# The first search of a routed expert layer in a written order, later routing steps, and weights requested in parts

## The chip, the cores and the metric

The kernel runs on one core of a Trainium2 chip. The metric is the device time of one execution in microseconds. Five engines work side by side, each through its own list of instructions in order: TensorE (PE; its weight loads are drawn apart as PEld), VectorE (DVE), ScalarE (ACT), GpSimd (POOL) and SyncE (SP), which issues most of the DMA transfers. They meet at semaphores.

## The reference

First a gated linear attention over q, k, v, alpha of 4 batches, 8 heads, 768 steps, head size 48:

```
state = alpha_t[:, None] * state + outer(k_t, v_t)      # 48 x 48 for each batch and head
y_t   = q_t @ state
```

Its output, laid out as x of 3072 tokens by 384, goes to a layer of 8 experts, each of which takes 384 tokens:

```
logits = x @ w_gate                                  # 3072 x 8
for idx in argsort(-logits.flatten()):               # best pair first
    tok, e = divmod(idx, 8)
    if assigned[tok] < 0 and counts[e] < 384: assigned[tok] = e; counts[e] += 1
out[mask_e] = relu(x[mask_e] @ w1[e]) @ w2[e]        # w1: 384 x 1024, w2: 1024 x 384
```

The assignment is greedy over 24,576 pairs. Which expert fills up first, and so which pairs are struck out, depends on the data.

## The kernel before

**Attention.** 24 steps (6 groups of 512 tokens by 4 pairs of heads) build the output channel by channel. Each result must be turned by four 128x128 transposes on TensorE (`y_trans`, L340), copied from PSUM by ScalarE into a tile `xg`, and stored to `x_dram` once a group of four steps is whole (L350). Eight of these 24 turnings are done by `fill` inside the attention part; sixteen are left.

**Routing.** In place of a sort the kernel finds, eight times, the expert that fills up next. `search` looks for the threshold key in five digits of 7, 7, 6, 6, 6 bits. A level compares all keys with all digit values (`compare`, the tables `cmp`, on VectorE), counts by expert with 24 small matmuls (`counts`), marks which digits reach the remaining capacity (`reached`), and sums the marks into the next digit (`flags`, whose result is `k`; then `next_digit`). `find` names the expert, and requests its weights on SyncE's queue with an address read from a register; `offsets` and `places` number its tokens; `one_hot` and `index` turn the numbers into a list of rows; `gather` brings the rows from `x_dram` by three indirect DMAs on GpSimd. `take_places`, `best_left`, `left` and `new_choice` strike the full expert out and choose anew. Level 0 of the first search is worked out during attention (`g0`).

**Order of the first search.** Attention is written under an order set by hand. The first `search(0)` is not: the planner orders it, with constraints that hold each level's counts behind the flag before and behind a given number of turnings (`Y_IN_SEARCH = (3, 4, 4, 3)`: 3, 4, 4 and 3 turnings, of four transposes each). All sixteen turnings come ahead of it in the program.

**Products.** Each expert makes 8 units `ffn1(i, q)` (9 matmuls of 384 columns, hidden block q) and 8 units `ffn2(i, [q])` (9 matmuls into three output banks): 144 products. Both operands are split into a high part on ScalarE (`split_hi`, `XH` in `rows`) and the rest on GpSimd (`split_lo`) or VectorE (`rows_lo`, `hl`), so each block takes three products. `rows(i, b)` turns the gathered block b of 128 tokens.

**The plan.** TensorE, VectorE, ScalarE and GpSimd run an order written out by hand. `products` gives the 1152 products one by one; a list `plan` says ahead of which product number each routing step of the next expert is written. Expert i's group of steps starts at `base`: 76 for i = 1, then 209, 342, 486, 630, 774 and 814, with 133, 133, 144, 144, 144 and 40 products between. From expert 2 on, the first unit of the expert is placed ahead of the last unit of the one before (L894). `spin_more` writes matmuls without a use, whose number is in `SPIN`.

**Weights.** `weights` requests the first half of an expert's w1 and w2 (four of eight hidden blocks) and, for all experts but the first, the other half at once. The first expert's other half is requested when its rows have landed (`second_half`).

Of the kernel before, what the change touches and what calls it, by code (L numbers as in the profile page):

```python
# [17 lines left out]
Y_IN_SEARCH = (3, 4, 4, 3)  # L18
SPIN = (16, 0, 4, 3, 3)
TRI = 11  # L20
HOT = 24
# [10 lines left out]
def gla_moe_kernel(ctx, tc, q, k, v, alpha, w_gate, w1, w2, out):  # L32
# [112 lines left out]
    NS = NG * HP  # L145
    psx = ctx.enter_context(tc.tile_pool(name="psx", bufs=1, space=bass.MemoryType.PSUM))
# [4 lines left out]
    pst = att.enter_context(tc.tile_pool(name="pst", bufs=1, space=bass.MemoryType.PSUM))  # L151
    ps = att.enter_context(tc.tile_pool(name="ps", bufs=1, space=bass.MemoryType.PSUM))
# [86 lines left out]
    def turned():  # L239
        turn[0] = not turn[0]  # L240
        return (psx if turn[0] else pst).tile([128, 4, C], F32, name="xt")

    turn = [False]
# [94 lines left out]
    YM = {}  # L338

    def y_trans(s):  # L340
        g, p = divmod(s, HP)
        o = turned()
        for u in range(4):
            YM[s] = nc.tensor.transpose(o[:, u], YT[s][:, u], ident)  # L344
        if p == 0:
            XG[g] = ytp.tile([128, 4, Dm], F32, name="xg", bufs=2)
        nc.scalar.activation(XG[g][:, :, 2 * D * p:2 * D * p + 2 * D].rearrange("p u (h d) -> p u h d", h=2),
                             o.rearrange("p u (h d) -> p u h d", h=2)[:, :, :, :D], AF.Copy)
        if p == HP - 1:
            nc.scalar.dma_start(x_dram[4 * g * C:4 * (g + 1) * C].rearrange("(u p) d -> p u d", p=C), XG[g])  # L350
# [68 lines left out]
    late = list(range(NS))  # L419

    def fill(n):
        for _ in range(min(n, len(late))):
            y_trans(late.pop(0))
# [62 lines left out]
    head = [NS - len(late)]  # L486
    fill(NS)
    att.close()

    rw = ctx.enter_context(tc.tile_pool(name="route_work", bufs=2))  # L490
    wp = ctx.enter_context(tc.tile_pool(name="weights", bufs=2))
    fp = ctx.enter_context(tc.tile_pool(name="ffn", bufs=2))
    fpt = ctx.enter_context(tc.tile_pool(name="ffn_pst", bufs=1, space=bass.MemoryType.PSUM))
    fps = ctx.enter_context(tc.tile_pool(name="ffn_ps", bufs=1, space=bass.MemoryType.PSUM))

# [14 lines left out]
    ab_c, q0_c, bi_c = slot(NU), slot(NU), slot(NU, I32)  # L510
    un_c, key_c, wi_c = ab_c, q0_c.bitcast(I32), v1_c.bitcast(I32)
    nc.vector.tensor_copy(ramp_c, ramp)
    nc.vector.tensor_copy(cst_c, cst)
# [12 lines left out]
    second_half = []  # L526

    def weights(i, ei):
# [4 lines left out]
        def half(hf):  # L533
            fs = slice(hf * F // 2, (hf + 1) * F // 2)
            a = nc.sync.dma_start(W1R[i][:, :, fs], w1v[bass.ds(ev, 1), :, :, fs].rearrange("e p c f -> p (e c) f"))
            qs = slice(hf * FB // 2, (hf + 1) * FB // 2)
            b = nc.sync.dma_start(W2R[i][:, qs], w2v[bass.ds(ev, 1), :, qs].rearrange("e p c d -> p (e c) d"))
# [18 lines left out]
    def halves(i):  # L556
        return [slice(0, NU // 2), slice(NU // 2, NU)] if i == 0 else [slice(0, NU)]
# [3 lines left out]
    last_k = [None]  # L561

    def search(i):
        chu, o, dig = st["chu"], st["o"], st["dig"]
        st["d"] = dig[0]
        for t, bits in enumerate(BITS):
            if t == 0:
                g = g0
            else:
                g = rw.tile([128, E], BF, name="g")  # L570
                final = t == nb - 1
                rt = st["rt"] = fps.tile([128, 64], F32, name="rt")
                cnt = rt[:, 32:40]
                head[0] += Y_IN_SEARCH[t - 1]
                order = [last_k[0], YM[head[0] - 1]]
                for cmp, js in compare(i, st["d"], t, final):
                    with ExitStack() as es_:
                        for x in order:
                            es_.enter_context(tc.issue_after(x.ins))
                        for j in range(js.start, js.stop):  # L580
                            nc.tensor.matmul(cnt, cmp[:, j // U, :, j % U], o[:, j], start=(j == 0), stop=(j == NU - 1))
                nc.vector.tensor_tensor(g, cnt, rem, op=OP.is_ge)
                if final:
                    keep_counts()
            if t == 0:
                st["rt"] = fps.tile([128, 64], F32, name="rt")
            st["g"] = g
            flags(t)
            if t < nb - 1:
                next_digit(t)  # L590

    def keep_counts():
        st["nt"] = nt = 2 ** BITS[-1]
        st["cs"] = rw.tile([128, E], F32, name="cs")
        nc.vector.tensor_copy(st["cs"][:nt + 1], st["rt"][:nt + 1, 32:40])

    def flags(t):
        rt = st["rt"]
        last_k[0] = nc.tensor.matmul(rt[:, :8], onet[t], st["g"], start=True, stop=True)
        st["k"] = rw.tile([128, 1], F32, name="k")  # L600
# [335 lines left out]
    with tc.manual_schedule(engines={E_.DVE, E_.PE, E_.Activation, E_.Pool}):  # L936
# [27 lines left out]
        for n in (3, 4):  # L964
            split_lo(0, n)
# [118 lines left out]
```

## Time and profile before

| | |
|---|---|
| median of 3 runs | 433.83 us (433.4 to 434.31) |
| profiled execution | 433.69 us, its span 431.8 us |
| TensorE busy | 396.6 us, 92% of the span |
| VectorE busy | 284.2 us, 66% |
| GpSimd busy | 279.9 us, 65% |
| ScalarE busy | 195.7 us, 45% |
| mean granted TensorE clock | 0.969 |
| last flag of the first search | 149.29 us |
| first product | 165.65 us |

Times in a profile row are the start from the span's beginning and the duration, in us. In a timeline row stand the start, the duration, the engine, the line of the kernel, the operation, the tiles (out<-in), shapes and a count; in brackets the idle time of the engine ahead of it and what ended it. A row with a count above one has several instructions merged. In a waits row stand who waited, for whom, the total in us, the times and the longest.

### The profile page before, as it was taken

How to read it: one execution, taken by the hardware profiler on the slowest of the kernel's cores; microseconds unless marked ns; L12 is line 12 of the kernel's file. 1: busy time of each engine (PE TensorE's matmuls, PEld its weight loads, DVE VectorE, ACT ScalarE, POOL GpSimd, SP SyncE). 2: the span in 40 equal slices, each digit the busy share in tenths (PEclk: the TensorE clock that was granted, in tenths of full speed). 3: DMA queues.
4: the chain of work that ended last, by engine and by line, in shares of the span. 5: the costliest groups of instructions: out<-in, count | busy, mean ns of one | idle time of the engine just before them, and what ended most of it. 6: DMA issues, size and time to landing. Idle time of an engine off the chain costs nothing.

```text
span 431.8 us, 10887 instructions
## 1 busy us (share of the span) xinstructions
PE 396.6 (92%) x4154; PEld 347.8 (81%) x4154; DVE 284.2 (66%) x838; ACT 195.7 (45%) x447; POOL 279.9 (65%) x327
## 2 busy tenths in 40 slices
PE   7999999989898858989999999999999997999993
PEld 3787777768676737989898899999999887999993
DVE  7888888878736497686697597687587576221210
ACT  1476666556565422424423534434434433644411
POOL 4668988677620026854687786776866865997802
PEclk9699999999999769999999999999999999999998
DMA  8999966660004584180180190191191198310101
GB/s 284 331 270 263 255 193 206 179 188 18 2 3 169 197 264 160 54 295 2 31 317 20 47 330 28 44 329 35 40 326 38 39 325 304 106 71 2 55 2 55
DMA packets 34467, 63.39 MB, mean 147 GB/s; under 512 B 3328, under 2 KB 14592, under 8 KB 34416
## 3 DMA queue, kind: packets, MB, share of 16 engines
q1 hardware_dynamic: 28176, 48.54, 36.0%
q0 software_dynamic: 3072, 9.44, 6.3%
q10 hardware_dynamic: 3168, 4.72, 3.1%
q8 instruction: 33, 0.54, 0.5%
q14 instruction: 18, 0.15, 0.1%
HBM read 53.25 MB, written 9.44 MB: 145 GB/s over the span
## 4 chain that ended last, share of the span: by engine, by line
PE 62%; DVE 21%; issue 6%; DMA 4%; POOL 3%; ACT 2%; SPq 0%; DVEq 0%; POOLq 0%; ACTq 0%
PE h L835 17%; PE y L855 16%; PE rt L614 6%; PE y L312 4%; PE y L306 4%; PE s L257 4%; DVE ga L226 3%; DVE sc L221 2%; DVE cmp L552 2%; PE xt L344 2%; DVE hot L699 2%; PE xt L249 2%; DMA raw_a<-in_alpha_dram 2%; PE xt L818 2%; PE xt L708 2%
## 5 line engine op out<-in xcount | busy, mean ns | idle before, releaser
L799 POOL TENSOR_TENSOR wlo<-w1r,whi 128x384 fp32r<-128x384 f32 x64 | 69.2, 1082 | 24.1 <-ACT whi L790 22.4
L799 POOL TENSOR_TENSOR wlo<-w2r,whi 128x384 fp32r<-128x384 f32 x64 | 68.0, 1063 | 25.6 <-PE xt L818 9.5
L840 ACT ACTIVATE hh<-h 128x384 fp32r<-128x384 f32 x64 | 31.5, 492 | 110.7 <-PE h L835 105.0
L841 DVE SCALAR_TENSOR_TENSOR hl<-h,hh 128x384 fp32r<-128x384 f32 x64 | 35.4, 553 | 51.8 <-ACT hh L840 50.6
L855 PE MATMUL y<-whi,hl 128*128 128x384 f32 x192 | 65.8, 343 | 0.0
L855 PE MATMUL y<-wlo,hh 128*128 128x384 f32 x192 | 65.8, 343 | 0.0
L855 PE MATMUL y<-whi,hh 128*128 128x384 f32 x192 | 64.9, 338 | 0.0
L716 POOL DMA_INDIRECT xr<-x_dram,idx x24 | 29.5, 1229 | 44.2 <-DVE asg L746 32.2
L269 POOL TENSOR_SCALAR_AFFINE_SELECT sm<-sm 128x512 f32<-128x512 f32 x48 | 29.4, 639 | 31.8 <-ACT sm L265 31.8
L835 PE MATMUL h<-xh,whi 128*128 128x384 f32 x192 | 47.5, 346 | 0.1
L835 PE MATMUL h<-xh,wlo 128*128 128x384 f32 x192 | 46.0, 344 | 0.0
L835 PE MATMUL h<-xl,whi 128*128 128x384 f32 x192 | 46.0, 344 | 0.0
L790 ACT ACTIVATE whi<-w1r 128x384 fp32r<-128x384 f32 x64 | 33.3, 520 | 25.0 <-PE y L855 10.8
L290 ACT ACTIVATE sb<-st,sc 128x48 f32<-128x48 f32 x80 | 24.6, 331 | 35.6 <-DVE st L297 21.2
L872 POOL DMA_INDIRECT out_dram<-yt,idx x24 | 25.0, 1043 | 18.4 <-ACT yt L859 14.6
L855 PEld LDWEIGHTS y<-whi,hl 128*128 128x128 f32 x192 | 36.2, 188 | 0.1
L855 PEld LDWEIGHTS y<-wlo,hh 128*128 128x128 f32 x192 | 36.2, 188 | 0.0
L855 PEld LDWEIGHTS y<-whi,hh 128*128 128x128 f32 x192 | 36.1, 188 | 0.0
L835 PEld LDWEIGHTS h<-xh,whi 128*128 128x128 f32 x192 | 33.6, 189 | 0.5 <-ACT xh L819 0.5
L835 PEld LDWEIGHTS h<-xh,wlo 128*128 128x128 f32 x192 | 33.8, 189 | 0.0
L552 DVE TENSOR_TENSOR cmp<-nd,iota 128x1536 bf16<-128x1536 bf16 (+4 forms) x32 | 33.1, 1044 | 1.0
L835 PEld LDWEIGHTS h<-xl,whi 128*128 128x128 f32 x192 | 33.6, 189 | 0.0
(177 smaller groups left out, 808.8 us busy)
## 6 DMA issues: line engine op xcount, KB each, us to landing
w1r<-in_moe_w_dram SPq DMA_DIRECT2D x16, 768.0 KB, 4.8
w2r<-in_moe_w_dram SPq DMA_DIRECT2D x16, 768.0 KB, 6.2
vt<-in_v_dram SPq DMA_DIRECT2D x24, 256.0 KB, 4.8
x_dram<-xg ACTq DMA_DIRECT2D x6, 768.0 KB, 3.7
raw_a<-in_alpha_dram SPq DMA_DIRECT2D x19, 226.2 KB
raw_k<-in_k_dram SPq DMA_DIRECT2D x19, 224.0 KB
raw_q<-in_q_dram SPq DMA_DIRECT2D x19, 224.0 KB, 5.2
raw_a<-in_alpha_dram SPq DMA_DIRECT2D x5, 258.5 KB, 5.0
```

Of the source, the lines that this page charges most:

```text
L269: nc.gpsimd.affine_select(SM[s][:, h], SM[s][:, h], pattern=[[0, 4], [1, C]], compare_op=OP.is_ge, fill=0.0, base=0, channel_multiplier=-1)
L290: nc.scalar.activation(SB[s, u][:, :D], St[p], AF.Copy, scale=ac)
L552: x = nc.vector.tensor_tensor(words(dst, nt, js), keyed(d, nt, js), each(iotas[t], nt, js), op=OP.is_ge)
L614: nc.tensor.matmul(rt[:, 32:40], st["cmp"][:, j // U, :, j % U], st["o"][:, j], start=(j == 0), stop=(j == NU - 1))
L716: g = nc.gpsimd.indirect_dma_start(out=XR[i][:, b], out_offset=None, in_=x_dram, in_offset=bass.IndirectOffsetOnAxis(ap=IDX[i][:, b:b + 1] ...
L790: nc.scalar.activation(hi[:, 0], a, AF.Copy)
L799: y = nc.gpsimd.tensor_sub(lo[:, h], x[h], hi[:, h])
L835: nc.tensor.matmul(o, a[:, 0, d], x[:, d], start=(n == 0), stop=(n == 3 * DB - 1))
L840: nc.scalar.activation(hh, o, AF.Relu)
L841: nc.vector.scalar_tensor_tensor(hl, o, 0.0, hh, op0=OP.max, op1=OP.subtract)
L855: nc.tensor.matmul(Y[b], a[:, bs], w[:, 1].rearrange("p a b -> p (a b)"), start=(q == 0 and n == 0), stop=(q == FB - 1 and n == 2))
L872: st_ = nc.gpsimd.indirect_dma_start(out=out, out_offset=bass.IndirectOffsetOnAxis(ap=IDX[i][:, b:b + 1], axis=0), in_=yts.pop((i, b)), in ...
```

## The change

It has five parts.

1. The first search is written into the hand-made order (`search_first`). A turning is now four steps of one transpose each (`y_steps`; the fourth brings the copy and, at the end of a group, the store). Three steps come ahead of each flag, 11, 8, 8 and 8 behind the flag and ahead of the counts of levels 1 to 4; the rest comes behind the last flag. The table is made in parts of 16 and 8 columns in place of 12 and 12. The tiles of the search lie in a pool of their own (`levels`), attention's tiles are let go only behind it, and `xg` has three buffers. The transposes alternate between `psx` and the bank of `y1`.
2. The bank `rt` of counts and flags is one tile throughout.
3. The first expert: two of eight blocks are split early in place of four, `spin_more` gives 16, 1, 1, 2 matmuls in place of 16, 4, 3, 3 (one more place had none), and level 0's flag and the steps behind it come after the third block of rows. The masking of `L` moves from `take_places`, ahead of the indices on VectorE, to `best_left`, behind them.
4. New positions: bases 98, 238, 382, 526, 670, 814, 872; other offsets for levels, places, one-hot, rows and splits. The table of level 0 comes behind `new_choice`. The first unit of an expert is no longer moved ahead of the last unit of the one before.
5. Weights: the first expert's come in parts of 2, 2 and 4 blocks, the others' in 4 and 4; all but the first part are requested when the expert's gathered rows have landed (`later`).

```
-Y_IN_SEARCH = (3, 4, 4, 3)
-SPIN = (16, 0, 4, 3, 3)
-TRI = 11
-HOT = 24
+Y_IN_LEVEL = (None, 11, 8, 8, 8)
+Y_BEFORE_FLAGS = 3
+SPIN = (16, 0, 1, 1, 2)
...
-        half(0)
-        if i:
-            half(1)
-        else:
-            second_half.append(half)
+        cuts = (0, 2, 4, FB) if i == 0 else (0, 4, FB)
+        part(*cuts[:2])
+        for lo, hi in zip(cuts[1:], cuts[2:]):
+            later.append((part, lo, hi))
...
+    def search_first():
+        st["d"] = st["dig"][0]
+        st["g"] = g0
+        steps(Y_BEFORE_FLAGS)
+        nc.vector.tensor_copy(ramp_c, ramp)
+        nc.vector.tensor_copy(cst_c, cst)
+        flags(0)
+        for t in range(1, nb):
+            next_digit(t - 1)
+            parts = list(compare(0, st["d"], t, t == nb - 1))
+            steps(Y_IN_LEVEL[t])
+            for cmp, js in parts:
+                for j in range(js.start, js.stop):
+                    nc.tensor.matmul(rt[:, 32:40], cmp[:, j // U, :, j % U], st["o"][:, j],
+                                     start=(j == 0), stop=(j == NU - 1))
+            reached(t)
+            steps(Y_BEFORE_FLAGS)
+            flags(t)
+        steps(4 * NS)
...
-            if i > 1:
-                units.insert(len(units) - 1, mine.pop(0))
...
+        if t == 0:
+            at(base + 11, rows_lo, i - 1, 1)
         if t < nb - 1:
-            at(base + 2, next_digit, t)
-            at(base + 2, table, i, t + 1)
+            at(base + (2 if t else 11), next_digit, t)
+            at(base + (2 if t else 11), table, i, t + 1)
...
-        levels(0, 1, {1: 1, 2: 9, 3: 21, 4: 36}, {})
-        found(39, 1, 37)
+    levels(0, 1, {1: 15, 2: 28, 3: 41, 4: 55}, {})
+    found(57, 1, 41)
...
-            loose = i > 2
-            offs = {0: 35, 1: 52, 2: 68, 3: 84, 4: 100} if loose else {0: 33, 1: 49, 2: 64, 3: 79, 4: 94}
-            end = 144 if loose else 133
+        offs = dict(enumerate((33, 56, 69, 83, 97) if i == 1 else (33, 57, 71, 85, 99)))
+        end = 140 if i == 1 else 144
...
-            at(base + 31, rows, i, 0)
-            at(base + (48 if loose else 45), rows, i, 1)
-            at(base + (60 if loose else 57), rows, i, 2)
+        for b, p in enumerate((31, 40, 46) if i == 1 else (31, 41, 50)):
+            at(base + p, rows, i, b)
...
-                at(base + 20, offsets, i + 1)
+            at(base + 34, offsets, i + 1)
```

More of the change, by code (lines that the diff above doesn't have):

```diff
@@ L417, in first @@
                                  ga[:, 129 * u:129 * u + 258].rearrange("p (g x) -> p g x", x=129)[:, :, 1:])
-    late = list(range(NS))
+    late = (x for s in range(NS) for x in y_steps(s))
     def fill(n):
-        for _ in range(min(n, len(late))):
-            y_trans(late.pop(0))
+        for _ in range(4 * n):
+            next(late, None)
     def run(seq):
@@ L485, in gla_moe_kernel @@
         first_counts(NG - 1)
[L486 to L493, printed above, removed]
+    first_psum.close()
     fps = ctx.enter_context(tc.tile_pool(name="ffn_ps", bufs=1, space=bass.MemoryType.PSUM))
+    spare_bank[0] = fps
     scr = fps.tile([128, 512], F32, name="scr")
@@ L556, in halves @@
     def halves(i):
-        return [slice(0, NU // 2), slice(NU // 2, NU)] if i == 0 else [slice(0, NU)]
+        return [slice(0, 2 * NU // 3), slice(2 * NU // 3, NU)] if i == 0 else [slice(0, NU)]
     st = dict(chu=chu0, o=o0, dig=[dig0[:, t] for t in range(nb)])
[L561 to L587, printed above, removed]
@@ L588, in search, with steps @@
             flags(t)
-            if t < nb - 1:
-                next_digit(t)
+        steps(4 * NS)
+    def steps(n):
+        for _ in range(n):
+            next(late, None)
     def keep_counts():
         st["nt"] = nt = 2 ** BITS[-1]
-        st["cs"] = rw.tile([128, E], F32, name="cs")
-        nc.vector.tensor_copy(st["cs"][:nt + 1], st["rt"][:nt + 1, 32:40])
+        st["cs"] = sm.tile([128, E], F32, name="cs")
+        nc.vector.tensor_copy(st["cs"][:nt + 1], rt[:nt + 1, 32:40])
     def flags(t):
-        rt = st["rt"]
@@ L718, in gather @@
                 in_offset=bass.IndirectOffsetOnAxis(ap=IDX[i][:, b:b + 1], axis=0))
-        for half in second_half:
-            for d_ in half(1):
+        for part, lo, hi in later:
+            for d_ in part(lo, hi):
                 tc.add_manual_dep(d_.ins, g.ins.name,
                                   mybir.DependencyInfo(mybir.DependencyClass.Sync, mybir.DependencyReason.DATA),
-                                  reason="rows of the first expert before its later weights")
-        second_half.clear()
+                                  reason="an expert's rows before its later weights")
+        later.clear()
     def take_places(i):
@@ new lines, in gla_moe_kernel @@
+    written = tc.manual_schedule(engines={E_.DVE, E_.PE, E_.Activation, E_.Pool})
+    written.__enter__()
+    search_first()
+    att.close()
+    rw = ctx.enter_context(tc.tile_pool(name="route_work", bufs=2))
+    wp = ctx.enter_context(tc.tile_pool(name="weights", bufs=2))
+    fp = ctx.enter_context(tc.tile_pool(name="ffn", bufs=2))
+    find(0)
+    offsets(0)
+    places(0)
+    one_hot(0)
+    index(0)
+    take_places(0)
+    gone()
+    spin_more(SPIN[0])
+    gather(0)
+    best_left(0)
@@ new lines, in gla_moe_kernel @@
+    left(0)
+    new_choice(0)
+    table(1, 0)
+    for q in range(2):
+        split_hi(0, q)
+    for n in range(3):
+        split_lo(0, n)
+    rows(0, 0)
+    counts(0)
+    rows_lo(0, 0)
+    reached(0)
+    spin_more(SPIN[2])
+    rows(0, 1)
+    rows_lo(0, 1)
+    spin_more(SPIN[3])
+    rows(0, 2)
+    flags(0)
+    rows_lo(0, 2)
+    next_digit(0)
+    table(1, 1)
+    split_hi(0, 2)
+    for n in (3, 4):
+        split_lo(0, n)
+    split_hi(0, 3)
+    spin_more(SPIN[4])
+    levels(0, 1, {1: 15, 2: 28, 3: 41, 4: 55}, {})
@@ L1044, with catch_up @@
+    plan.sort()
+    waiting, made = [], products()
+    def catch_up():
+        waiting[:] = [(fn, args) for fn, args in waiting if fn(*args) is False]
+    for n in range(2 * E * FB * NB * DB):
+        while plan and plan[0][0] <= n:
+            waiting.append(plan.pop(0)[2:])
+        catch_up()
+        next(made)
+    for _ in made:
+        pass
+    catch_up()
+    assert not waiting and not plan
+    written.__exit__(None, None, None)
 _INS = ["q", "k", "v", "alpha", "moe_w_gate", "moe_w1", "moe_w2"]
```

232 lines of the change are left out of this document (91 added, 141 removed).

## The prediction

> **What bounds the kernel now.** I read the page first, then the busy time by stage, then TensorE's waits in the expert stage, then the timeline of the stretch between attention and the first product.
>
> ```profile
> span 431.8 us, 10887 instructions
> ...
> L841 DVE SCALAR_TENSOR_TENSOR hl<-h,hh 128x384 fp32r<-128x384 f32 x64 | 35.4, 553 | 51.8 <-ACT hh L840 50.6
> ...
> x_dram<-xg ACTq DMA_DIRECT2D x6, 768.0 KB, 3.7
> ```
>
> The profiled execution took 433.69 us, 0.14 under the median of the three runs; its span is 431.8, so 1.9 us lie around it. Sums below are made against 433.69.
>
> Busy time by stretch (PE, PEld, DVE, ACT, POOL, then the granted clock, DMA share, GB/s):
>
> ```profile
> 140.00:142.00 2.00, 2.00 (x31) 1.94 (x31) 0.17 (x1) 0.91 (x2) 0.00 (x0) 0.50 0.93 332
> ...
> 152.00:154.00 2.00, 0.00 (x0) 0.00 (x0) 1.83 (x8) 0.00 (x0) 0.00 (x0) 0.60 1.03 319
> ...
> 134.05:149.29 15.24, 13.63 (x157) 11.58 (x156) 7.66 (x24) 6.66 (x14) 0.00 (x0) 0.78 0.51 182
> 149.29:165.65 16.36, 10.30 (x97) 6.90 (x95) 13.53 (x51) 5.82 (x13) 5.99 (x6) 0.79 0.71 219
> ...
> 285.00:318.00 33.00, 32.82 (x307) 30.49 (x305) 24.16 (x74) 13.61 (x30) 24.38 (x26) 1.00 0.38 129
> ```
>
> Three stages matter. The first search (134 to 149) runs partly at half clock, TensorE busy with transposes. From 149 to 166 VectorE sets the pace (13.5 of 16.4 us busy). After that TensorE does: one expert's 33 us hold 32.8 of it. So whatever moves there counts only through TensorE's waits, and these are few:
>
> ```profile
> PE rt L663 <- DVE rts L653: 2.7, 1, 2.7
> PE rt L659 <- DVE rts L640: 2.1, 3, 1.1
> PE xt L708 <- DVE rhs L701: 1.5, 3, 0.7
> PE rt L614 <- DVE cmp L552: 1.3, 3, 0.7
> PE xt L818 <- DVE rem L775: 0.6, 1, 0.6
> PE xt L708 <- DVE xl L824: 0.3, 1, 0.3
> PE xt L818 <- DVE xl L824: 0.2, 1, 0.2
> PE xt L818 <- DVE chu L769: 0.2, 1, 0.2
> ```
>
> That is 14 waits, 8.9 us idle. A product is drawn as some 0.34 us but they start 0.173 apart, so each wait hides another 0.17: 8.9 + 14 x 0.17 = 11.3 us in all. This is the most that new positions can win after 165.65.
>
> **The search (gain 2.5).** Each level runs: flag k, next digit, table, 24 count matmuls, reached, flag.
>
> ```profile
> 134.67 0.17 DVE L601 TENSOR_REDUCE k<-rt 128x1 f32<-128x8 f32 x1 [0.18 <-issue]
> ...
> 137.88 3.00 PE L344 MATMUL xt<-ident,yt 128*128 128x128 f32 x13
> 138.06 0.17 DVE L601 TENSOR_REDUCE k<-rt 128x1 f32<-128x8 f32 x1 [0.26 <-PE rt L599]
> ...
> 142.46 0.17 DVE L601 TENSOR_REDUCE k<-rt 128x1 f32<-128x8 f32 x1 [0.61 <-PE rt L599]
> ...
> 144.28 0.72 PEld L344 LDWEIGHTS xt<-ident,yt 128*128 128x128 f32 x4 [0.26 <-ACT xg L347]
> ...
> 146.62 0.17 DVE L601 TENSOR_REDUCE k<-rt 128x1 f32<-128x8 f32 x1 [0.26 <-PE rt L599]
> ...
> 147.82 0.94 PE L581 MATMUL rt<-o,cmp 128*128 128x8 bf16 x24
> ...
> 149.09 0.86 PEld L344 LDWEIGHTS xt<-ident,yt 128*128 128x128 f32 x8 [0.40 <-ACT xg L347]
> 149.29 0.17 DVE L601 TENSOR_REDUCE k<-rt 128x1 f32<-128x8 f32 x1 [0.26 <-PE rt L599]
> ```
>
> From k to k the four levels take 3.39, 4.40, 4.16 and 2.67 us. In the two slow ones 13 transposes stand ahead of the counts, at half clock. The last has few ahead of it and full clock: 2.67 is what the bare chain costs. The change puts 11, 8, 8, 8 transposes ahead of the counts and 3 ahead of each flag. Eight take 0.86 at full clock (the last weight-load row) and 2 x 0.72 = 1.44 at half; between flag and ready table lie some 1.3 us (2.67 less the counts' 0.94 and 0.4 from there to the flag), so at half clock they stick out by 0.1, and the 3 ahead of the flag (0.54 against some 0.3 that it waits anyway) by 0.25. I take 3.2 for the first level (its table is twice as long, and its second part now the shorter), 3.1, 3.1 and 2.7: 12.1 against 14.62, a gain of 2.5. The clock window could fall otherwise: at full clock throughout 3.2 + 3 x 2.67 = 11.2, a gain of 3.4. If banks or copies hold the transposes up as before in one level, 1.2 is left. The third bank set for the rows (xg) only helps.
>
> Fourteen transposes are left behind the last flag. They lie beside VectorE's chain of small operations, but their last store is now asked for some 2.3 us after k (four copies of some 0.5 after each other), not 1.45 (150.74, below).
>
> **From the search to the first product (gain 0.9).**
>
> ```profile
> 150.74 0.37 ACTq L350 DMA_DIRECT2D x_dram<-xg  x1
> ...
> 156.01 0.16 DVE L713 TENSOR_SCALAR idx<-xt 128x3 int32<-128x3 f32 x1 [0.26 <-PE xt L708]
> ...
> 157.14 1.16 POOL L716 DMA_INDIRECT xr<-x_dram,idx  x1 [32.17 <-DVE asg L746]
> ...
> 160.21 1.75 DVE L552 TENSOR_TENSOR cmp<-top,iota 128x3072 bf16<-128x3072 bf16 x1
> ...
> 161.94 0.52 PE L818 MATMUL xt<-ident,xr 128*128 128x128 f32 x3 [1.48 <-DMA xr<-x_dram,idx]
> ...
> 162.30 0.93 PE L614 MATMUL rt<-o,cmp 128*128 128x8 bf16 x24
> ...
> 163.09 0.81 PE L882 MATMUL y<-warm 128*128 128x384 bf16 x4
> ...
> 164.57 0.49 PE L818 MATMUL y<-ident,xr 128*128 128x128 f32 x3
> ...
> 165.10 0.49 ACT L819 ACTIVATE xh<-y 128x384 fp32r<-128x384 f32 x1 [0.35 <-PE y L818]
> ...
> 165.65 0.44 PE L835 MATMUL h<-xh,whi 128*128 128x384 f32 x1
> ```
>
> The store lands 3.7 us after its issue, so 6.0 after k, while the indices are ready 6.7 after k: not late, though only by 0.7. The weights asked for ahead of the rows are two blocks of eight, not four, so the rows, now 4.8 us from issue to use, come sooner; but the counts wait for VectorE's table (till 161.96) anyway. That table moves by -0.15 (a last part of 8 one-hot columns, not 12, 0.034 us each) and by +0.38 (the masking of L comes after the indices), so the counts start level with before, 0.1 earlier. Behind them stand 2 spins where there were 7, and 2 more after the last rows hide in the 1.08 us between those transposes (164.57) and the first product (165.65). Five spins of some 0.16 (four took 0.81 with the tail of the last) are 0.8: 0.9 in all. Weights for the third and fourth block come behind the rows, at about k + 17; their first product is at k + 19.5 at least: hidden, with 2 us of cover, and if the rows were late by more, each further us would be a stall.
>
> **The expert stage (loss 0.2).** Counting positions in products, routing of expert 2 onward starts 22 to 40 products later, with longer gaps for the search's last steps. Gone: all 11.3. The largest, 2.7, goes because the last expert's offsets stand 22 products (3.8 us) behind their start, not 8. New waits:
>
> ```profile
> 284.45 0.34 DVE L730 SCALAR_TENSOR_TENSOR L<-scr,L 128x192 f32<-128x192 f32 x1
> ...
> 285.52 0.16 DVE L713 TENSOR_SCALAR idx<-xt 128x3 int32<-128x3 f32 x1 [0.73 <-PE xt L708]
> ...
> 291.89 0.17 DVE L776 SCALAR_TENSOR_TENSOR rem<-scr,rem 128x8 f32<-128x8 f32 x1
> ...
> 292.45 0.96 PE L614 MATMUL rt<-o,cmp 128*128 128x8 bf16 x24
> ...
> 400.21 1.53 ACT L859 ACTIVATE yt<-y 128x384 f32<-128x384 f32 x3
> ```
>
> - Last rows: bases are 98, 238, 382, 526, 670, 814, and the third block's transposes stand at base + 46 or + 50: 144, 288, ... 864, right ahead of that expert's first product, which reads all three blocks and, for experts from 2 on, no longer stands ahead of the last output unit of the expert before. So TensorE waits for the copy: 1.08 us from transposes to product, of which 0.36 is their own time, plus 0.1 because ScalarE is still at the three output copies (1.53). 0.8 x 6 experts = 4.8.
> - First table: VectorE's chain from indices to rem took 6.4 us, then the counts at + 35. Now it has L's 0.38 more and the counts stand at + 33 (0.35 sooner); a wait of 0.2 + 0.17 ahead of them (the last row of the waits) is gone too. The old slack was 0.4 (292.06 to 292.45), so 0.7 for experts 2 to 5, 2.8. At expert 1 a subtraction hl (0.55), itself waiting for ScalarE, gets ahead of the whole chain: 1.5.
> - Expert 1's rows follow at 31, 40, 46, closer than VectorE's release of the bank: 0.5.
> - Index of the second and third expert: hl stands ahead of the one-hot (some 1.75, like the table of the same size): 0.4 + 0.9.
> - First expert: 0.5 (its table, its low parts); last: 0.1.
>
> Together 11.5, against 11.3. Both ends: if VectorE's chain hides the table and index waits, 5.8 remain (gain 5.5); if each boundary costs what the rival below says, 16. The weights behind the rows (asked at some base + 7 us, first read at base + 86 products, 15 us and more) cost nothing; SyncE alone waits there, and nothing else is queued on it. The single rt tile, seven output tiles in place of five and the later splitting of the first blocks cost nothing: ScalarE is busy 13.6 of 33 us.
>
> **Sum.** 433.69 - 2.5 - 0.9 + 0.2 = 430.5.
>
> **Rivals.**
>
> *A, positions pay.* The steady experts show only 0.2 us idle in 33, and the new waits were worked out from program order, not seen. If only the boundaries stay, 433.69 - 3.4 - 5.5 = 424.8; with half of the others 427.6, which I take.
>
> *B, slower at the boundary.* The third block's low part (subtracted on VectorE) stands behind the second digit's table, 1.75 us. I have it ready as the seventh product of the expert needs it. That product waits as soon as table or flag slips; 1.75 shows no slack. One more table part of 0.9 for each of five experts is 4.5: 435.0. It decides from 0.65 us for each (3.2 / 5). For: VectorE is 24 of 33 busy. Against: the wait ahead of the first product gives it 0.8 of cover.
>
> *C, half clock at the first products.* Spins go from 10 to 4, and granted clock was 0.50 in 140 to 142 and fell within 152 to 154, after idle. One such stretch lasted some 6.8 us; half of it lost is 3.4: 433.9. Against: the 16 spins stay, and products are dense from the start.
> The Trainium skill, "TensorE: Matmul & The Clock Gate", section "Why this matters for your kernels", asks for no idle gap over about 3 us between bursts of matmuls, or the clock halves; by it this rival is live, since transposes and counts with gaps fill the time before. The trace agrees after the idle stretch from 150 (0.60 in 152 to 154).
>
> *D, the search doesn't shorten.* Transposes wait for copies and the store goes later than the indices, so the front gives 0.5 in place of 3.4: 433.4. For: the 0.7 us of slack. Against: two banks and a copy of 0.5 for each four.
>
> **How the numbers follow.** 0.48 forecast, 0.24 A, 0.10 B, 0.08 C, 0.10 D. 0.2% (0.87 us) is what a measurement can tell from none. The forecast and A are faster; C and D mostly the same, B slower: 0.75, 0.14, 0.11. The forecast's own range is 428.8 to 432.2 (search 1.2 to 3.4, waits by 1); with A below and C and D above, 426.5 to 434.2 leaves out 2 in 10.
>
> **What would show it.** k to k at about 3.2, 3.1, 3.1, 2.7; first product some 3.4 earlier; ahead of each expert's first product a wait for ScalarE's xh of about 0.8; a wait of the first counts for the table; none for the last offsets. I am wrong if those waits are absent or over 1.5 each, or if the granted clock is half after the first product.

## The result, and the profile after

The kernel after takes 437.57 us (median of 4 runs, 436.55 to 438.54), the kernel before 433.62 us (4 runs, 433.40 to 434.31) beside it: the ratio is 1.0088, 95% interval 1.0062 to 1.0115. It is slower, and the forecast of 430.5 was wrong in its sign. The profiled execution after took 436.55 us, 2.86 more than that of before. A ratio, here and below, is worked out from all runs of a set but one at 484.68 us in `k1_front_new`, and differs a little from the quotient of the two medians.

From the page of the kernel after, one group (busy us and mean ns, then idle time and what ended it):

```profile
L818 PE MATMUL h<-xh,whi 128*128 128x384 f32 x192 | 46.7, 348 | 3.7 <-ACT xh L801 3.7
```

The group's wait is new: 3.7 us of TensorE's idle time ahead of a product, which waits for `xh`. Busy time by stretch in the kernel after (PE, PEld, DVE, ACT, POOL, granted clock, DMA share, GB/s): the search, from its last flag to the first product, the first expert's 144 products, products 144 to 1008, the rest, and, in the last row, one expert (products 576 to 720) by itself:

```profile
134.72:146.29 11.57, 10.49 (x149) 8.35 (x146) 7.29 (x22) 5.50 (x12) 0.00 (x0) 1.00 0.56 205
146.29:162.78 16.49, 11.91 (x96) 7.63 (x95) 12.98 (x51) 5.31 (x12) 5.98 (x6) 0.72 0.62 198
162.78:200.28 37.50, 34.22 (x307) 31.34 (x306) 25.33 (x76) 13.64 (x31) 18.64 (x19) 0.99 0.47 156
200.28:402.62 202.34, 193.71 (x1683) 179.23 (x1684) 130.35 (x386) 80.44 (x181) 135.53 (x152) 1.00 0.39 130
402.62:434.81 32.19, 25.12 (x145) 24.80 (x144) 4.46 (x8) 10.08 (x23) 17.88 (x24) 0.93 0.10 37
...
305.22:340.02 34.80, 33.41 (x307) 30.70 (x307) 24.80 (x75) 13.37 (x31) 22.73 (x25) 1.00 0.36 114
```

The same stretches of the kernel before, cut at the same products:

```profile
165.65:203.67 38.02, 35.62 (x357) 32.36 (x357) 28.33 (x84) 12.97 (x29) 24.16 (x23) 1.00 0.39 136
203.67:399.49 195.82, 189.22 (x1634) 177.89 (x1634) 126.30 (x380) 82.49 (x183) 147.61 (x155) 1.00 0.38 134
399.49:431.77 32.28, 25.12 (x145) 24.80 (x144) 4.46 (x8) 8.66 (x18) 11.89 (x18) 0.96 0.10 37
...
306.89:339.69 32.80, 32.79 (x308) 30.72 (x307) 24.12 (x75) 13.62 (x30) 24.45 (x26) 1.00 0.39 133
```

Up to product 144 the kernel after is 3.39 us ahead (200.28 against 203.67). Then 864 products take 202.34 us in place of 195.82: 6.52 lost. The rest is alike: 6.52 - 3.39 - 0.09 after product 1008 - 0.18 around the span = 2.86. By expert, the starts of products 144, 288, 432, 576, 720, 864 and 1008 lie 35.31, 34.79, 33.13, 32.79, 34.35 and 25.45 us apart before, and 35.29, 34.79, 34.86, 34.80, 35.13 and 27.48 after. Before, the first two steps and the one that carries the last offsets stand well above 32.8; after, each of the first five does, by 2.0 or more. The first two steps are as long as before, so the 6.52 us are lost from product 432 on (1.73, 2.01, 0.78 and 2.03 in the last four steps). TensorE's waits in the product stage of the kernel after (who waited, for whom, us in all, times, longest):

```profile
PE rt L600 <- DVE cmp L547: 4.3, 9, 1.2
PE h L818 <- ACT xh L801: 3.7, 6, 0.6
PE rt L586 <- DVE g L605: 1.3, 1, 1.3
PE xt L800 <- DVE xl L806: 0.9, 2, 0.7
PE xt L800 <- issue: 0.7, 1, 0.7
PE xt L691 <- DVE rhs L684: 0.7, 1, 0.7
PE h L818 <- POOL wlo L782: 0.2, 1, 0.2
```

The wait for the last offsets' `rts` is gone, and so are those for the other offsets; six waits for `xh` have come, and nine for a table where there were three. The front, in the timeline of the kernel after (start, duration, engine, line, operation):

```profile
134.72 0.16 DVE L588 TENSOR_REDUCE k<-rt 128x1 f32<-128x8 f32 x1
...
137.97 0.17 DVE L588 TENSOR_REDUCE k<-rt 128x1 f32<-128x8 f32 x1 [0.26 <-PE rt L586]
...
140.92 0.17 DVE L588 TENSOR_REDUCE k<-rt 128x1 f32<-128x8 f32 x1 [0.26 <-PE rt L586]
...
143.57 0.17 DVE L588 TENSOR_REDUCE k<-rt 128x1 f32<-128x8 f32 x1 [0.26 <-PE rt L586]
...
146.29 0.17 DVE L588 TENSOR_REDUCE k<-rt 128x1 f32<-128x8 f32 x1 [0.26 <-PE rt L586]
...
159.45 0.96 PE L600 MATMUL rt<-o,cmp 128*128 128x8 bf16 x24 [0.86 <-DVE cmp L547]
...
162.78 1.28 PE L818 MATMUL h<-xh,whi 128*128 128x384 f32 x3
```

The four levels take 3.25, 2.95, 2.65 and 2.72 us, at full clock; the first product is 2.87 us earlier than before.

### The profile page after: what moved, and what is told of

It is laid out like the page before. It is cut to its first block, busy times and chain, and to the rows that moved or that the text cites. A ratio compares the mean times of both kernels' runs of the same rounds, so it can differ in the third digit from the quotient of the medians.

```text
span 434.8 us, 10871 instructions
## 1 busy us (share of the span) xinstructions
PE 397.6 (91%) x4148; PEld 345.5 (79%) x4148; DVE 284.4 (65%) x836; ACT 193.9 (45%) x447; POOL 268.5 (62%) x327
## 4 chain that ended last, share of the span: by engine, by line
PE 59%; DVE 22%; issue 6%; DMA 4%; ACT 4%; POOL 3%; SPq 0%; ACTq 0%; DVEq 0%; POOLq 0%
PE h L818 16%; PE y L838 15%; PE rt L600 5%; PE y L314 4%; PE y L308 4%; PE s L259 4%; DVE cmp L547 3%; DVE ga L227 2%; PE xt L251 2%; DVE sc L222 2%; DMA raw_a<-in_alpha_dram 2%; DMA w2r<-in_moe_w_dram 2%; PE xt L691 2%; DVE hl L824 2%; PE st L281 2%
## 5 line engine op out<-in xcount | busy, mean ns | idle before, releaser
L782 POOL TENSOR_TENSOR wlo<-w2r,whi 128x384 fp32r<-128x384 f32 x64 | 64.9, 1014 | 35.2 <-DVE cmp L547 27.4
L782 POOL TENSOR_TENSOR wlo<-w1r,whi 128x384 fp32r<-128x384 f32 x64 | 64.8, 1012 | 23.1 <-ACT whi L773 17.7
L838 PE MATMUL y<-whi,hh 128*128 128x384 f32 x192 | 66.0, 343 | 0.0
L699 POOL DMA_INDIRECT xr<-x_dram,idx x24 | 23.1, 964 | 56.0 <-DVE asg L729 29.4
L818 PE MATMUL h<-xh,wlo 128*128 128x384 f32 x192 | 47.1, 345 | 0.2 <-POOL wlo L782 0.2
L855 POOL DMA_INDIRECT out_dram<-yt,idx x24 | 28.1, 1170 | 12.4 <-ACT yt L842 8.5
L600 PEld LDWEIGHTS <-cmp 128*128 128x128 bf16 x720 | 26.3, 118 | 11.2 <-DVE cmp L547 8.2
L547 DVE TENSOR_TENSOR cmp<-nd,iota 128x1536 bf16<-128x1536 bf16 (+7 forms) x32 | 33.7, 1064 | 1.0
```

Of the source, the lines that this page charges most:

```text
L547: x = nc.vector.tensor_tensor(words(dst, nt, js), keyed(d, nt, js), each(iotas[t], nt, js), op=OP.is_ge)
L600: nc.tensor.matmul(rt[:, 32:40], st["cmp"][:, j // U, :, j % U], st["o"][:, j], start=(j == 0), stop=(j == NU - 1))
L699: g = nc.gpsimd.indirect_dma_start(out=XR[i][:, b], out_offset=None, in_=x_dram, in_offset=bass.IndirectOffsetOnAxis(ap=IDX[i][:, b:b + 1] ...
L782: y = nc.gpsimd.tensor_sub(lo[:, h], x[h], hi[:, h])
L818: nc.tensor.matmul(o, a[:, 0, d], x[:, d], start=(n == 0), stop=(n == 3 * DB - 1))
L838: nc.tensor.matmul(Y[b], a[:, bs], w[:, 1].rearrange("p a b -> p (a b)"), start=(q == 0 and n == 0), stop=(q == FB - 1 and n == 2))
```

## The experiments

The kernel before was timed again with each set of runs. Its medians there were 435.07 to 435.6 us, single runs from 432.5 to 438.7, so each ratio is against the kernel before of the same set. The kernel after itself was timed only in the set of the result (1.0088, 1.0062 to 1.0115), so the ratio of a variant of it is set against one from another set; what one mend is worth is read from its profile instead, by the times between products, from product 144 on at a granted clock of 1.00 unless said otherwise. "New front" is parts 1 to 3 of the change without the move of `L`'s masking, and the first expert's weights in parts.

**New front, old positions, whole weights** (`k1_front_new`): part 4 and part 5 (from the second expert on) undone, `L` masked where it was.

```
-            later.append((part, lo, hi))
+            if i:
+                part(lo, hi)
+            else:
+                later.append((part, lo, hi))
...
-    levels(0, 1, {1: 15, 2: 28, 3: 41, 4: 55}, {})
...
+    levels(0, 1, {1: 1, 2: 9, 3: 21, 4: 36}, {})
...
```

All else of the plan is as before, too.

> The changed kernel's front (first search in the written order, first expert's order, its weights in parts of 2, 2 and 4 blocks) with the positions, the order of product units, the mask of L and the whole weights of the other experts as before. Theory P (the new positions cost 6 us through TensorE's waits, the front saves 3): 433.6 - 3 = 430.6, first product near 162.8, index to index 33.0. Rival W (the weights in parts behind the rows cost it): 430.6 too. Rival F (an earlier front is given back later, since the first expert's weights land no sooner): near 433.5, with new waits between 163 and 186.

Measured: 436.8 us, ratio 1.0024 (0.9993 to 1.0056): no gain. Products 144 to 1008 are as long as before, to 0.83 us:

```profile
205.47:402.12 196.65, 189.55 (x1634) 178.04 (x1634) 126.26 (x380) 82.45 (x183) 148.21 (x155) 1.00 0.39 133
```

So 5.7 of the 6.5 us belong to what is undone here. But the front alone doesn't pay either: its first product starts at 163.47, product 144 only at 205.47. Two causes can be seen: a wait of 2.1 us in TensorE for the second level's table (the old positions put its counts one product behind the first, and the table is not made that early), and half clock from 164.8 to 175.0.

**Weights whole** (`k5_weights_whole`): the kernel after, other weights than the first expert's requested when found.

> The changed kernel with one part undone: experts 1 to 7 request all their weights when they are found, as before. Theory P: no difference beyond 0.9 us from the changed kernel, about 437.6, since rows are read only at base + 31 products. Rival W: the waits of ScalarE for landing weights (6.9 us in the changed kernel) go, and with them most of the 4 us: 433 to 434.

Measured: 437.92 us, 1.0061 (1.0038 to 1.0084); products 144 to 1008 take 202.51 us. Part 5 costs these experts nothing and wins nothing.

**The spins** (`k6_front_new_spins`: the kernel of k1 with `SPIN = (16, 0, 4, 3, 3)`; `k8_few_spins`: the kernel before with `SPIN = (16, 0, 1, 1, 2)`).

> The kernel with the new front and the old positions, now with the spins of before (16, 0, 4, 3, 3 in place of 16, 0, 1, 1, 2). Theory C (the shorter spins let the clock fall to half among the first products, which took 10 us there in the run without them): no half clock after the first product, products 0 to 144 in 38 us in place of 42, and 431.5 in all. Rival G (the half clock comes from the search's own windows, whatever the spins): half clock again between 160 and 175, and 434 to 437.

> The kernel before with one number changed: spins 16, 0, 1, 1, 2. Theory C: the first product comes 0.8 earlier, and half clock for 3.4 to 10 us follows behind it, so 434 to 438. Rival G: 0.8 faster, about 432.8.

Measured: k6 435.59 us, 1.001 (0.9987 to 1.0033); k8 435.25 us, 1.0014 (0.9992 to 1.0036). The spins do nothing that can be measured in all. In k8's profile the stretch from the last flag to the first product takes 15.70 us (148.52 to 164.22) where the kernel before took 16.36, but product 144 starts at 203.59 against 203.67. In its profile k6, with the spins of before, still has half clock from 168.3 to 175.1, and its first expert's products take

```profile
163.57:204.80 41.23, 37.84 (x356) 34.10 (x357) 28.73 (x84) 14.83 (x33) 24.12 (x23) 0.92 0.44 149
```

where the kernel before took 38.02.

**The search alone** (`k9_search_alone`): the kernel before with parts 1 and 2 only; the first expert's order, spins and weights as before.

> The kernel before with the written search alone (its order, its pools, its parts of 16 and 8 columns); the first expert's order, its 10 spins, the weights, the place of L's masking and all positions as before. Theory S (the search is worth what it saves): the last flag some 3 us earlier, first product at 163.0 to 163.5, product 144 at 201.0 to 201.5 against 203.67, median some 2.4 below the kernel before, ratio 0.9945. Theory H (the half clock takes it): the last flag is as early, but a half-clock stretch of 3.4 to 6.8 us falls behind the first product in place of ahead of it, product 144 at 203 to 205, ratio 0.998 to 1.002.

Measured: 434.52 us, 0.9992 (0.997 to 1.0014): nothing. Product 144 starts at 204.75, as theory H has it, though by another way. The search takes 11.56 us (135.97 to 147.53), and then the rows are late. The split of the weights that are asked for last ahead of the rows, and the first rows, in its timeline:

```profile
160.64 0.52 ACT L777 ACTIVATE whi<-w2r 128x384 fp32r<-128x384 f32 x1 [2.72 <-DMA w2r<-in_moe_w_dram]
...
161.25 0.52 PE L803 MATMUL xt<-ident,xr 128*128 128x128 f32 x3 [2.09 <-DMA xr<-x_dram,idx]
```

TensorE turns the first rows 25.28 us after the first flag, in the kernel after 23.35 (158.07 less 134.72), where two blocks of weights are asked for ahead of them, not four. The first product is at 167.1, where k6, with the smaller first request and the first expert's new order, has it at 163.57. In these two traces the earlier search reaches the first product only with them; k6 as a whole is no faster either.

**Blocks of rows earlier** (`k3_rows_early`), on the kernel after:

```
-            at(base + 11, rows_lo, i - 1, 1)
+            at(base + 8, rows_lo, i - 1, 1)
...
-        for b, p in enumerate((31, 40, 46) if i == 1 else (31, 41, 50)):
+        for b, p in enumerate((31, 37, 41) if i == 1 else (31, 38, 45)):
...
-            for b, p in enumerate((35, 45, 54)):
+            for b, p in enumerate((35, 42, 49)):
```

> The changed kernel with the second and third block of rows 3 to 5 products earlier (31, 38, 45 in place of 31, 41, 50; 31, 37, 41 in place of 31, 40, 46 for expert 1), so that five products stand between the last transposes and the product that reads them. Theory P: the waits for xh (3.7 us idle in 6, 0.8 each from start to start) go: 437.6 - 4 = 433.6. If TensorE then waits for the bank ahead of the transposes in their place: no more than 1.5 us gained, 436.

Measured: 436.39 us, 1.0037 (1.0009 to 1.0065). The waits for `xh` go, and the step of an expert (products 576 to 720) falls by 0.55, not 0.8:

```profile
305.32:339.57 34.25, 33.48 (x307) 30.54 (x307) 24.80 (x75) 13.36 (x31) 22.78 (x25) 1.00 0.35 113
```

Most of it is given back at the end: products 720 to 1008 take 64.43 us where the kernel after takes 62.61, since TensorE waits longer ahead of the seventh expert's rows (2.4 us in two waits, for 1.4) and then 0.9 for a low weight and 0.6 for the bank of the last expert's rows. Products 144 to 1008 win only 0.62.

**L's masking ahead of the indices again** (`k4_mask_back`), on the kernel after.

> The changed kernel with the mask of L ahead of the indices again, as before. Theory P: VectorE's chain from indices to the first table is 0.38 shorter in five experts, so the wait of 0.64 ahead of the first counts falls to 0.3: 437.6 - 1.5 = 436.1, if what follows isn't VectorE's too; rival: the wait only moves to the second table, 437.6.

Measured: 437.82 us, 1.0069 (1.0048 to 1.0089), though the step of an expert falls to 34.41 and products 144 to 1008 take 200.83 us, 1.5 less, as theory P has it: four of the five waits for the first level's table go or shrink to 0.1. The median doesn't show it. Its profile has half clock in the first expert (174.2 to 177.7), where the kernel after has it for 1.1 us only (0.99 there).

**The seventh expert's rows ahead of the last one-hot** (`k10_rows_first`), on the kernel after:

```
-            for b, p in enumerate((35, 45, 54)):
+            for b, p in enumerate((33, 44, 54)):
...
-            at(base + 40, one_hot, i + 1)
+            at(base + 46, one_hot, i + 1)
```

> The kernel after; of the seventh expert only, the low parts of its first two blocks are subtracted two and one product earlier and the last expert's one-hot is written six products later, so that VectorE has both low parts behind it before the one-hot (1.75 us). Theory P (new waits cost what they show): the two waits of TensorE for xl, 0.9 each, go; products 720 to 1008 take 60.8 us against 62.6; median 435.8 for 437.6, ratio to the kernel before 0.995 lower than the kernel after has. Rival M (waits move): the one-hot is late in turn, the index of the last expert waits 0.9 or more, 62.0 to 62.6.

Measured: 436.25 us, 1.0038 (1.0011 to 1.0066). Products 720 to 1008 of the kernel after:

```profile
340.01:402.62 62.61, 60.09 (x459) 56.57 (x460) 31.32 (x90) 26.96 (x61) 48.68 (x58) 1.00 0.46 155
```

and of k10:

```profile
340.74:401.55 60.81, 59.62 (x460) 56.63 (x460) 30.75 (x90) 26.84 (x61) 48.72 (x58) 1.00 0.47 160
```

1.80 us less, as theory P said; the ratio to the kernel before is 0.5% lower than that of the kernel after, though the two intervals touch.

**Counts later** (`k11_counts_later`), on the kernel after:

```
-        offs = dict(enumerate((33, 56, 69, 83, 97) if i == 1 else (33, 57, 71, 85, 99)))
+        offs = dict(enumerate((33, 56, 69, 83, 97) if i == 1 else (38, 62, 74, 87, 100)))
```

> The kernel after with the levels of the experts from the third on written 5, 5, 3, 2 and 1 products later (38, 62, 74, 87, 100 in place of 33, 57, 71, 85, 99). Theory P: the waits of the counts for the first table (0.64) and the second (0.45) go with their restarts, the step from one expert to the next falls from 34.8 to 33.5 us, median 433 to 434, four such experts. Rival V (VectorE's chain of an expert is too long for what is left of it): the wait comes back at the index or the next rows, the step stays within 0.4 of 34.8, median 436.5 or more.

Measured: 438.45 us, 1.0065 (1.0039 to 1.009). One expert takes 34.55 us, and its waits are

```profile
PE xt L691 <- DVE rhs L684: 0.7, 1, 0.7
PE h L818 <- ACT xh L801: 0.6, 1, 0.6
```

where the same stretch of the kernel after has

```profile
PE rt L600 <- DVE cmp L547: 0.7, 2, 0.5
PE h L818 <- ACT xh L801: 0.6, 1, 0.6
```

The waits for the tables have become one for the one-hot, as rival V says. Room given in one place was taken from the next, since the expert's index still stands at 144. The tables that were waited for are the first and the third level's, not the second's, as is shown below.

**Low parts of hidden blocks later** (`k13_after_hl_later`): each `hl` is written four products later.

> The kernel after, with each hidden block's low part (hl, on VectorE) written four products later, so that VectorE doesn't stand in its queue waiting for ScalarE's hh while routing steps are ready behind it. Theory Q (the routing steps are late because hl, itself waiting, is ahead of them in VectorE's order): the waits for tables, flag and one-hot (4.3, 1.3 and 0.7 us) fall to a third, the step of one expert from 34.8 to 34.0, median 433.5 to 434.5. Rival V (VectorE's own work is what is late): steps stay within 0.3 of 34.8, median 437 or more.

Measured: 436.7 us, 1.0031 (1.0002 to 1.0059); products 144 to 1008 take 202.44 us, the step stays 34.8, as rival V has it. But the waits move as theory Q says: those for the flag and the one-hot are gone, and so are the four ahead of the third level's counts (products 309, 453, 597 and 741). The five that are left (2.4 us) stand ahead of the first level's counts. In place of what went, products wait 2.1 us for `hl` itself.

**Three mends together** (`k16_after_mended`): k3, k4 and k10 in one kernel.

> The kernel after with the three mends that have been run alone put together: blocks of rows earlier (38, 45 and 42, 49), L's masking ahead of the indices, the low parts of the seventh expert ahead of the last one-hot. Theory P (the new waits add up): the step of one expert falls by 0.57 and 0.40 to 33.85, the last steps by 1.8, products 144 to 1008 take 196.6 us against 202.3, as long as the old positions do, median 433.5. Rival V (waits move): step 34.2 or more, 198.5 or more, median 435 or more.

Measured: 433.59 us, 0.9972 (0.9941 to 1.0003). The step, and products 144 to 1008:

```profile
304.82:338.72 33.90, 33.47 (x308) 30.55 (x307) 24.79 (x75) 13.38 (x31) 22.79 (x25) 1.00 0.36 118
...
202.99:400.75 197.76, 193.90 (x1685) 178.28 (x1684) 129.36 (x386) 81.15 (x183) 136.53 (x153) 1.00 0.40 133
```

In the step the mends add up, as theory P says (0.57 + 0.40 gives 33.85). At the end they don't: products 720 to 1008 take 62.03 us against 62.61, where 1.8 less was expected, with new waits of 0.8 us for rows to land and 0.6 for the bank. In all 4.58 of the 6.52 us come back, and the ratio can't be told from 1.

**The last expert's offsets later, in the old plan** (`k2_last_later`): of the new positions only those of the last expert's offsets, one-hot and index.

```
-                at(base + 20, offsets, i + 1)
-                at(base + 20, places, i + 1)
-                at(base + 26, one_hot, i + 1, 1)
-                end = 40
+                at(base + 34, offsets, i + 1)
+                at(base + 34, places, i + 1)
+                at(base + 40, one_hot, i + 1, 1)
+                end = 58
```

> The kernel before with the last expert's offsets, one-hot and index at base + 34, 40 and 58 in place of 20, 26 and 40, as the changed kernel has them. Theory P: the wait of 2.9 us ahead of those offsets goes; products 720 to 1008 take 57 us in place of 59.8, and 431 in all, if the rows of expert 6 (at 31, 48, 60) don't wait for VectorE in its place as they do in the changed kernel at 31, 41, 50 (0.9 twice). Rival: the two waits come here too, 432.5.

Measured: 433.32 us, 0.9947 (0.992 to 0.9973): faster. Products 720 to 1008 take 57.7 us in place of 59.8. With the front of k6 (`k7_front_spins_last`):

> Both: the new front with the old spins, the old positions, and the last expert's steps later. If the parts add: 2.2 from the front and 2.5 from the last expert, 429. If the clock falls to half in the first products all the same: 431 to 434.

Measured: 432.16 us, 0.9935 (0.9903 to 0.9967); the front's share can't be told from none.

**More room for the first three experts, in the kernel of k7** (`k12_best`).

> The kernel with the new front, 10 spins and the last expert's later offsets, and beside these the waits of the kernel before taken away in the first three experts by a few products more room each: the second expert's search at 12, 21, 31, 42 in place of 1, 9, 21, 36; bases 82, 218, 356 in place of 76, 209, 342; offsets 13 and one-hot 27 products behind the find in place of 11 and 24. Theory P: the waits for the second table (2.1), the offsets (2.0) and the one-hot (1.5) go for the most part, 4 us in all, median 428 to 429, ratio 0.984. Rival V: they move to the rows' release and the low parts, median 431 to 432, ratio 0.992.

Measured: 436.94 us, 1.0032 (1.0003 to 1.006), a plain miss of both theories. Of the 4.1 us between its profile and that of k7, 3.2 are lost up to product 144 (44.4 us at a clock of 0.88, for 41.1 at 0.92): the wait for the second table falls from 2.1 to 0.9, but a flag now waits 2.6. Behind, the steps from product 432 to 576 and to 720 take 34.39 and 34.13 us in place of 33.17 and 32.79, with one wait in each:

```profile
PE rt L647 <- DVE rts L629: 1.1, 1, 1.1
```

The positions of these experts' steps to one another are unchanged; only the base stands 14 products later against their products.

**Low parts later, in the kernel of k7** (`k14_hl_later`).

> The kernel with the new front, 10 spins and the last expert's later offsets (432.16 us), with each hl written four products later. Theory Q: the waits for the offsets' sums (2.0) and the one-hot (1.5) in the first three experts go, products 144 to 720 take 132.5 us against 136.05, median 429, ratio 0.986. Rival V: 135.5 or more, median 431.5 to 432.5, ratio 0.993.

Measured: 430.4 us, 0.9899 (0.9867 to 0.9931): the lowest median of all, though the interval overlaps that of k7. Its waits from product 144 to 1008:

```profile
PE xt L694 <- DVE rhs L687: 1.4, 2, 0.8
...
PE rt L647 <- DVE rts L629: 0.2, 1, 0.2
```

The waits for the offsets' `rts`, 2.0 us in k7, fall to 0.2; those for the one-hot stay. Theory Q holds for the offsets; products 144 to 720 take 134.33 us, between the 132.5 of theory Q and the 135.5 of rival V.

**TensorE kept busy** (`k15_spins_dense`): k7 with 13 more spins behind `offsets(0)` and 9 behind the first product.

> The same kernel (432.16 us) with 22 more matmuls without a use where TensorE stands idle: 13 behind the first offsets (149.5 to 152.8) and 9 behind the first product (163.9 to 166). Theory C2 (half clock comes some 3.4 us after a stretch in which TensorE is idle for more than a third): both half-clock stretches, 151.4 to 158.2 and 168.4 to 175.2, go; product 144 at 201.0 to 202.0 against 205.0, median 429.5. Rival R (the spins don't count, or the clock falls for another reason): half clock stays behind the first product, product 144 at 204 to 206, median 432 to 433.

Measured: 431.49 us, 0.9923 (0.9895 to 0.995), not to be told from k7. In its profile the first expert's products run at full clock,

```profile
166.50:205.61 39.11, 37.34 (x367) 33.30 (x366) 28.73 (x84) 14.83 (x33) 24.11 (x23) 0.99 0.42 144
```

2.0 us shorter than in k7 (41.14 at 0.92), but there the half clock fell on the search (139.6 to 149.8) and on the stretch up to the first product (160.1 to 166.9) instead, and product 144 starts at 205.61, in k7 at 205.03. Neither theory is settled by it.

## Why the prediction was wrong

**The search: right.** 2.5 was forecast; 11.57 us against 14.62 is 3.05. The levels took 3.25, 2.95, 2.65 and 2.72 where 3.2, 3.1, 3.1 and 2.7 were forecast: the half clock that the working left on the middle ones was not there in this execution, which is luck in part: in k15, with the same written search, half clock came from 139.6 to 149.8, and the levels took 3.24, 3.30, 3.31 and 3.31, 13.16 in all, a gain of 1.5.

**Search to first product: wrong by its size.** The 0.9 was not won: 16.49 us against 16.36. The counts wait for the table as forecast, 13.16 us after the last flag (before 13.01). Five spins fewer should then have saved 0.8, but the clock was half from 160.46 to 163.87, 1.1 us past the first product: the transposes of the second and third block of rows take 0.81 and 0.85 us there, 0.49 before. In k8, with fewer spins and nothing else, this stretch is 0.66 shorter. A small term was off besides: the working has a column of one-hot at 0.034 us, but before 12 columns took 0.95 us and 24 took 1.75, which is 0.067 a column. In all the first product came 2.87 earlier, not 3.4. k9 adds what the working had passed over: it gave the smaller first request of weights no part in the time, and in k9, without it, the search's gain is lost to rows that land late.

**What was removed: right.** The waits for `rts` went (2.7 and 2.1). k2 shows the last expert's offsets alone to be worth 0.5%.

**The new waits: the step that failed.** 11.5 us were forecast. From the first product to the last the kernel after needs 6.0 us more than the one before, so with 11.3 removed the new waits are 17.3. Term by term:

- Boundary, 0.8 x 6: 3.7 us in 6 waits and 0.17 hidden in each, 4.7. Right; k3 shows that the place of the third block causes it.
- First tables, 0.7 x 4 and 1.5 at the second expert: waits of 0.47 to 0.49 and 0.17 hidden in each, 0.64 x 4, and the longest wait for a table, 1.2 and 0.17: 3.9 for 4.3. Right; k4 takes most of it away.
- Third tables, forecast at nothing: 0.28 and 0.17 in each of four experts, 1.8. In the timeline of the kernel after:

```profile
303.97 1.76 DVE L547 TENSOR_TENSOR cmp<-nd,iota 128x3072 bf16<-128x3072 bf16 x1
...
306.55 0.96 PE L600 MATMUL rt<-o,cmp 128*128 128x8 bf16 x24
...
307.82 0.18 PE L586 MATMUL rt<-g,one 128*128 128x8 bf16 x1
...
308.54 0.56 DVE L824 SCALAR_TENSOR_TENSOR hl<-h,hh 128x384 fp32r<-128x384 f32 x1 [0.81 <-ACT hh L823]
...
309.01 0.15 DVE L588 TENSOR_REDUCE k<-rt 128x1 f32<-128x8 f32 x1
...
309.48 0.96 DVE L547 TENSOR_TENSOR cmp<-nd,iota 128x1536 bf16<-128x1536 bf16 x1
...
310.49 0.97 PE L600 MATMUL rt<-o,cmp 128*128 128x8 bf16 x24 [0.28 <-DVE cmp L547]
```

The second level's table is done 0.8 us ahead of its counts (306.55). Its flag's matmul starts at 307.82, but VectorE reads it only 1.19 us later (0.23 in the next level, 311.76 to 311.99): an `hl` stands ahead, and this one itself waits 0.81 us for ScalarE's `hh`. So the third table and the counts behind it are late. k13 shows the cause: with `hl` written four products later, none of these four waits is left.
- The seventh expert's rows, forecast at nothing: 0.7 and 0.7 with 0.17 each, 1.7. The last expert's one-hot is written on VectorE ahead of the low parts that free the bank for the next block. This gave back much of the 2.7 won at the last offsets; k10 gets 1.8 back.
- Index of the second and third expert, 1.3: one wait, 0.7 and 0.17. Expert 1's rows, 0.5: 0.2 and 0.17.
- The first expert, forecast at 0.5: one wait of 1.3 for a flag. In the timeline of the kernel after:

```profile
170.57 0.52 ACT L774 ACTIVATE whi<-w2r 128x384 fp32r<-128x384 f32 x1 [1.48 <-DMA w2r<-in_moe_w_dram]
...
171.00 0.47 ACT L823 ACTIVATE hh<-h 128x384 fp32r<-128x384 f32 x1
...
171.50 0.56 DVE L824 SCALAR_TENSOR_TENSOR hl<-h,hh 128x384 fp32r<-128x384 f32 x1 [1.97 <-ACT hh L823]
...
172.19 0.17 PE L586 MATMUL rt<-g,one 128*128 128x8 bf16 x1 [1.30 <-DVE g L605]
```

ScalarE stands at the split of a late weight, `hh` behind it, `hl` behind that on VectorE, and the flag behind `hl`. The 2 us of cover that the working gave the weights behind the rows were not enough here. No run changes this alone (in k13 the wait is gone, but half clock up to 171.4 had held the products back there), so it is a reading of one trace.

So the terms that the working listed come to 11.4 against 11.5, the first expert's 1.0 more made up by less elsewhere, which is partly luck. What failed is what it put at nothing: the third tables (1.8), the seventh expert's rows (1.7) and a wait for a low weight (0.2 and 0.17), 3.9 together. The 21 waits of the list are 15.4 in this count; the other 1.9 of the 17.3 are in no wait of the list, and where they lie is not shown. k16 checks part of the reading: three mends, aimed at the boundary, the first tables and the seventh expert's rows, bring products 144 to 1008 to 197.76 us, where k1's old positions need 196.65. The third tables' waits are still in it (0.3 in its step).

**The rivals.** A had the sign wrong. B had the sign right and VectorE's lateness, but another place and size: no product waits for a third block's low part, and the second digit's table is on time; the third's is late, by 0.45 in four experts where B put 0.9 in five. D, no gain from the front, is what the medians of k1, k6 and k9 look like, but by other causes: late rows, a late second table, half clock. C's cause, fewer spins, falls (k6, k8); its price doesn't. The same work has the half clock in some executions without any of the change: in the profile of the kernel before products 0 to 144 took 38.02 us at a clock of 1.00, and in k2, which has the same work up to there,

```profile
165.45:206.08 40.63, 38.21 (x357) 34.71 (x357) 28.48 (x84) 12.97 (x29) 24.13 (x23) 0.92 0.36 126
```

2.6 us more at 0.92. The forecast was made against a profile without it.

**What stays open.** Why 14 products' shift of the base costs two experts 1.2 and 1.3 us in k12 when the steps keep their distances; that `hl` stands in the way of the offsets is shown for the first experts (k14) and not for these. Where the 1.9 us without a wait lie. And what would keep the clock full.

## What to carry to other kernels

In an order written by hand, work out for each step whether the engine that prepares it has done so by that position, with everything that is queued ahead on that engine and what that waits for itself, before moving it: here a small step that was ready stood behind an `hl` that waited 0.81 us for a third engine. A stage that shows no waits is already well placed against its neighbours, and moving all of it cost each round 2 us here, while the one long wait (here the last offsets) can be mended alone. A faster front is worth only what the transfers behind it allow: take its gain at the first product and again a hundred products later.

## What the runs showed of the hardware

Half clock comes without a long idle stretch too. In k7, which has the old spins, 6.8 us of half clock follow 3.4 us in which TensorE was busy less than six tenths:

```profile
165.00:168.40 3.40, 1.98 (x31) 1.83 (x32) 1.95 (x5) 1.67 (x4) 1.89 (x2) 1.00 0.91 284
168.40:175.20 6.80, 6.80 (x62) 5.68 (x61) 3.49 (x7) 2.02 (x5) 3.58 (x5) 0.50 0.43 160
```

Its longest wait from 163 on is 2.1 us:

```profile
PE rt L603 <- DVE cmp L550: 2.3, 2, 2.1
```

The Trainium skill, "TensorE: Matmul & The Clock Gate", section "Why this matters for your kernels", asks that idle gaps stay under about 3 us; here half clock came with shorter ones, so the rule is not enough. k6 shows the same in the middle of the products: behind the wait of 2.7 us for the last offsets (ended at 359.26) it has

```profile
359.43:362.84 3.41, 3.41 (x12) 3.31 (x13) 3.20 (x10) 0.49 (x1) 0.00 (x0) 0.50 0.88 297
```

where the profile of the kernel before stays at full clock behind the same wait. That is some 1 us of products 720 to 864 (35.35 us against 34.35), and k8 and k9 have it too (35.29 and 35.42). In k15 half clock followed 132.8 to 139.6, where TensorE was busy 5.50 of 6.80 us at full clock:

```profile
132.80:139.60 6.80, 5.50 (x65) 4.11 (x64) 5.38 (x17) 3.71 (x8) 0.00 (x0) 1.00 0.59 217
139.60:149.80 10.20, 10.20 (x110) 9.44 (x109) 5.16 (x22) 3.93 (x8) 0.00 (x0) 0.50 0.49 177
```

That stretch is transposes and counts of 8 columns. Whether these count as busy for the clock was not tested.
